# A random-feature attention with a routed two-layer network: h read once per block, y read one block later, a rewoven last step, and one-hots laid out in steps of one

## The chip, the cores and the metric

The kernel runs on one core of a Trainium2 chip. The metric is the device time of one execution in microseconds (us), as the median of several runs. TensorE is called PE in the profile, VectorE DVE, ScalarE ACT, GpSimd POOL and SyncE SP. "Line numbers" such as L926 are lines of the kernel before.

## The reference

Two stages. The first is attention with random features, for 8 batches, 8 heads, 576 positions and head dimension 64, with 128 features; its output, laid out as 4608 rows of 512, is the input of the second, a mixture of 8 experts of which each row takes the best one.

```python
def phi(x):
    proj = np.einsum('bhsd,md->bhsm', x, omega)
    return np.concatenate([np.cos(proj), np.sin(proj)], axis=-1) / np.sqrt(m)
q_p, k_p = (phi(q), phi(k))
kv = np.einsum('bhsm,bhsd->bhmd', k_p, v)
z = np.sum(k_p, axis=2)
num = np.einsum('bhsm,bhmd->bhsd', q_p, kv)
den = np.einsum('bhsm,bhm->bhs', q_p, z)
x = (num / den)            # 4608 rows of 512
...
logits = xn @ en.T / tau   # rows and expert embeddings normed
expert_idx = np.argmax(logits, axis=1)
gate_w = softmax(logits)[row, expert_idx]
for e in range(8):
    mask = expert_idx == e
    h = np.maximum(x[mask] @ w1[e], 0.0)          # 512 -> 1024
    out[mask] = gate_w[mask, None] * (h @ w2[e])  # 1024 -> 512
```

## The kernel before

**Attention loop.** There are 32 steps (a batch and a pair of heads each), software-pipelined by hand in the loop over n at L1067: step n makes the features of its own q (`proj_q`, L269; `whole_turns`, `frac`, `fold`, `wave`), the k features of step n+1 (`proj_k`), the sums of k features on POOL (`zsum`, L315), the products kv (`kv_products`, L327), and finishes step n-1: `kv_copy`, `kv_turn` (L350), `kv_out` (copy L374), `num` (L380, products L389) and `norm` (L397). `to_rows` and `store_rows` write the rows x to DRAM; `sums` (L455), `squares`, `square_sums` and `square_rows` (L444) prepare logits and norms. The loop runs to n = 32, where only the finishing half is left. Inside a step the order in each engine's queue is the order of the calls.

**Routing.** Rows are sorted by expert into blocks of 128 rows. This is done twice: once for the first half of the batches during steps 18 to 30 (`route_first`, L1009; its pieces go through a small holding list, `release`), giving blocks 0 to 10, and once for the rest while blocks 0 to 6 run (`route_second`, L1173, and `route_second_pe`). A routing goes: `choose`, `choose2` (best expert), `scan` (running counts), `rank` (two products, L632 and L633), `places` to `places3` (each row's block and row within it), `block_hot` and `row_hot` (one-hots of these), `invert` (36 products, L722, in the second one, that turn row numbers into a list of rows per block), `rows_of` and `block_experts`. Gates (`gates_a` to `gates_d`, with a tanh on ACT) are stored beside the rows. Most DVE operations of the routing have the helper's line: L153 in the blocks, L177 where they were held.

**Blocks.** Block j: `gather` (L819, an indirect DMA from POOL, issued four blocks ahead, three buffers) fetches the rows; `turn_x` transposes them on PE with a copy by ACT for blocks 0 to 2, and `turn_x_dma` (L856, from SP's queue) by DMA from block 3 on; `turn_x` also copies the gate (L852). `hidden(j)` (L921) makes h in two PSUM banks with 32 products L926, 16 for each bank, and ACT applies relu to each bank in an instruction of its own (L934, L936). `result(j)` (L941) makes y in one bank with 8 products L947, and ACT reads it with the gate as scale (L967). `scatter(j)` (L972, an indirect DMA from POOL) writes the rows of y to the output. h uses banks 4, 5 or 0, 1 and y bank 3 or 7, by the parity of j. The weights' addresses depend on the block's expert: PE holds them in 48 registers, which `place` (L908) sets by register adds, between the products of `result`.

`block` (L1223) calls, in this order: `hidden(j+1)`, `route_second_pe`, `turn_x(j+2)`, `turn_x_dma(j+3)`, `route_second`, `gather(j+4)`, `result(j)`, `scatter(j)`. So PE's queue has h of the next block in front of y of this one. 40 blocks are run always; the last 3 stand in a branch that this input doesn't take. `scatter(38)` and `scatter(39)` come after the branch.

The pieces that the change touches at the end of the loop:

```python
if n < NS:                      # L1085
    proj_q(n, place_first if n == NS - 1 else lambda: None)
...
if n == NS:                     # L1101
    hidden(0, "act")
if n > 0:
    kv_turn(n - 1)
    kv_out(n - 1)
release(100.0)
if n == NS:
    place(1, range(NW1))
```

`place_first` (48 adds) runs between the two groups of products of the last `proj_q`. In step 31 `route_first` also holds `choose(2)`, `square_rows(2)`, `choose2(2)`, which `release(100.0)` lets out after `kv_out`. The first gather is issued at the start of step 31, the gathers 1 to 3 at its end.

Of the kernel before, what the change touches and what calls it, by code (L numbers as in the profile page):

```python
# [28 lines left out]
def kernel(  # L29
# [12 lines left out]
    nc = tc.nc  # L42
# [95 lines left out]
    with tc.tile_pool(name="psA", bufs=1, space=PSUM) as psA, tc.tile_pool(  # L138
# [130 lines left out]
        def proj_q(n, between=lambda: None):  # L269
            d = st[n]  # L270
            for par in range(2):
                r0 = 64 * par
                nc.tensor.matmul(  # L273
                    qreg[:, 512 * par : 512 * par + 512],
                    lhsT=omT[r0 : r0 + 64],
                    rhs=d["qT"][r0 : r0 + 64, P:],
                    start=True,
                    stop=True,
                )
            between()  # L280
            nc.tensor.matmul(  # L281
                qreg[:, 1024:1152],
                lhsT=omT[64:P],
                rhs=d["qT"][64:P, 0:P],
                start=True,
                stop=True,
            )
# [414 lines left out]
        def block_hot(blk, ns, k0, nk, ar):  # L702
            bm = ar.take(ns * nk, BF16).rearrange("p (s k) -> p s k", k=nk)
            rr = ar.take(ns * nk * 2, BF16).rearrange("p (s t k) -> p s t k", t=2, k=nk)
            shp = [P, ns, nk]
            rv.tensor_tensor(
                bm, bc(io_p[:, k0 : k0 + nk], shp, 1), bc(blk, shp, 2), ALU.is_equal
            )
            rv.tensor_tensor(rr[:, :, 0], bm, bc(tok_hi[:, 0:ns], shp, 2), ALU.mult)
            rv.tensor_tensor(rr[:, :, 1], bm, bc(tok_lo[:, 0:ns], shp, 2), ALU.mult)  # L710
            return rr

        def row_hot(oh, lo, a, b):
            shp = [P, b - a, P]
            rv.tensor_tensor(
                oh[:, a:b], bc(io_p, shp, 1), bc(lo[:, a:b], shp, 2), ALU.is_equal
            )

        def invert(oh, rr, ns, nk, inv):
            inv = inv[:, 0 : 2 * nk]  # L720
            for s in range(ns):
                nc.tensor.matmul(  # L722
                    inv,
                    lhsT=oh(s),
                    rhs=rr[:, s].rearrange("p t k -> p (t k)"),
                    start=(s == 0),
                    stop=(s == ns - 1),
                )
            return inv
# [191 lines left out]
        def hidden(j, eng):  # L921
# [12 lines left out]
            nc.scalar.activation(hT[:, 0:512], h_ps[:, 0:512], AF.Relu)  # L934
            if eng == "act":
                nc.scalar.activation(hT[:, 512:], h_ps[:, 512:], AF.Relu)  # L936
            else:
                nc.vector.tensor_scalar(hT[:, 512:], h_ps[:, 512:], 0.0, None, ALU.max)
            d["hT"] = hT

        def result(j):  # L941
# [4 lines left out]
            for c in range(NW2):  # L946
# [14 lines left out]
                elif c == 6 and 0 < j < NBLK - 1:  # L961
                    place(j + 1, [NW1 + NW2 * ((j + 1) % 2) + 7])
            if j < NBLK - 1:
                y = late("si" + "kq"[j % 2], j // 2 % 2, 2 * D).bitcast(FP32)
            else:
                y = late("coq", 0, 2 * D).bitcast(FP32)
# [3 lines left out]
        ys = {}  # L970
# [38 lines left out]
        def route_first(n):  # L1009
# [43 lines left out]
            elif m == 12:  # L1053
                gates_d(0, GRP1)
                store_gates(0, GRP1)
            elif m == 13:
                choose(GRP1)
                square_rows(GRP1)
                choose2(GRP1)
# [7 lines left out]
        for n in range(NS + 1):  # L1067
# [13 lines left out]
            if n == NS - 1:  # L1081
                gather(0)
            if 0 < n <= n1 + 2:
                nc.tensor.addr_align(128, STEP_AT)
            if n < NS:  # L1085
                proj_q(n, place_first if n == NS - 1 else lambda: None)
# [13 lines left out]
            release(0.9 if n < NS - 1 else 0.0)  # L1100
            if n == NS:  # L1101
                hidden(0, "act")
# [3 lines left out]
            release(100.0)  # L1106
            if n == NS:
                place(1, range(NW1))
            if nx:
# [6 lines left out]
            if n > 2:  # L1116
# [7 lines left out]
            if n >= NS - 1:  # L1124
                turn_x(n + 1 - NS, "act")
# [17 lines left out]
            if n < NS:  # L1143
                kv_products(n)
                wave(n, "si", "q")
                wave(n, "co", "q")
            if n > 0:
                norm(n - 1)
            if n == NS - 2:
                load_v(n + 1)  # L1150
            route_pool(n)
            if n == NS - 1:
                gather(1)
# [8 lines left out]
        r2 = {}  # L1162

# [9 lines left out]
        def route_second(j):  # L1173
            if j == 0:
# [18 lines left out]
                )  # L1193
                choose(NGRP - 1)
                choose2(NGRP - 1)
                scan()
            elif j == 1:
                squares(NS - 1, nc.vector)
# [9 lines left out]
            elif j == 3:  # L1208
                r2["rr"] = block_hot(r2["blk"], NSLOT, K1, NBLK - K1, r2["a"])
            elif j == 4:  # L1210
                for a in range(0, 18, 6):
                    row_hot(r2["oh"][0], r2["lo"][:, 0:18], a, a + 6)
            elif j == 5:
                for part in (gates_a, gates_b, gates_c, gates_d):
                    part(GRP1, NGRP)
                store_gates(GRP1, NGRP)
                for a in range(0, 18, 6):
                    row_hot(r2["oh"][1], r2["lo"][:, 18:36], a, a + 6)
# [4 lines left out]
        def block(j, end):  # L1223
            if j + 1 < end:
                hidden(j + 1, "act")
# [12 lines left out]
            if not LAST - 2 <= j < LAST:  # L1238
                scatter(j)
# [6 lines left out]
        with tc.If(nb > LAST):  # L1246
            turn_x(LAST, "act")
            hidden(LAST, "act")
# [41 lines left out]
```

## Time and profile before

| what | before |
|---|---|
| median of 3 runs | 482.73 us (482.70, 482.73, 485.98) |
| the profiled execution | 485.38 us, span 483.5 us, mean granted PE clock 0.986 |
| attention loop, to the last num | 0 to 320.3 us |
| result(0) to result(7), start to start | 323.30 to 354.70 us |
| result(7) to result(39), start to start | 354.70 to 472.4 us |
| tail | the last product ends at 474.3 us, the span at 483.5 us |
| busy time | PE 456.8, PE weight load 379.5, POOL 367.2, ACT 340.3, DVE 294.7 us |

Times are of one profiled execution on the only core. In a timeline a row has start, length, engine, line, operation, output and inputs with their shapes and the number of instructions merged, and in brackets the idle time of the engine ahead of it with what ended it; "issue" means that the profile shows nothing that it waited for. Two blocks without a pause are 7.03 us (2 x 3.515).

### The profile page before, as it was taken

The page shows a single profiled execution, that of the slowest core. Times are in us where ns is not written, and L with a number is a line of the kernel's source. Part 1 is how long each engine was busy: PE and PEld are TensorE (multiplying, and loading weights), DVE is VectorE, ACT ScalarE, POOL GpSimd, SP SyncE. Part 2 cuts the span into 40 slices and gives each one's busy share as a digit, 9 for nine tenths or more (in the row PEclk, how much of TensorE's full clock was granted, in tenths as well). Part 3 has the DMA queues.
Part 4 walks back from the last instruction along what each step waited for, and adds up shares of the span by engine and source line. Part 5 has one row for each costly group of instructions (what it writes and reads, how often), then busy time and mean ns, then how long its engine had stood idle before and what let it go on. Part 6 is the DMA issues. An engine that isn't in the chain of part 4 may idle for free.

```text
span 483.5 us, 18511 instructions
## 1 busy us (share of the span) xinstructions
PE 456.8 (94%) x7778; PEld 379.5 (78%) x7778; DVE 294.7 (61%) x523; ACT 340.3 (70%) x439; POOL 367.2 (76%) x472
## 2 busy tenths in 40 slices
PE   8999999999999999999999899889899999999992
PEld 7888888898898888888888798767577676666660
DVE  4689888799888789989888988769710000000000
ACT  3878888888888889899889789464345354453541
POOL 3799888889999999989999789768645554645543
PEclk9999999999999999999999999899989999999997
DMA  6499798798887888897888868335636455454531
GB/s 179 103 186 205 170 173 167 186 166 163 176 165 144 204 165 160 164 169 168 166 160 184 153 143 130 64 66 136 137 97 145 136 116 138 122 131 137 125 95 35
DMA packets 77715, 70.46 MB, mean 146 GB/s; under 512 B 49461, under 2 KB 57653, under 8 KB 77632
## 3 DMA queue, kind: packets, MB, share of 16 engines
q0 software_dynamic: 18064, 30.96, 34.2%
q1 hardware_dynamic: 59168, 37.80, 32.6%
q8 instruction: 64, 1.05, 0.9%
q10 hardware_dynamic: 400, 0.49, 0.4%
q14 instruction: 19, 0.16, 0.1%
HBM read 67.90 MB, written 15.22 MB: 172 GB/s over the span
## 4 chain that ended last, share of the span: by engine, by line
PE 39%; POOL 27%; issue 19%; DVE 6%; DMA 4%; ACT 3%; POOLq 1%; SPq 0%; ACTq 0%; DVEq 0%
PE ps L389 11%; PE ps L335 9%; POOL xin_all L821 7%; PE ps L227 5%; PE ps L261 5%; POOL zt L322 4%; PE ps L273 4%; POOL out_dram L974 4%; DMA out_dram<-sik,prm 3%; POOL zt L323 2%; POOL zs L324 2%; POOL zs L325 2%; PE ps L364 2%; PE ps L356 2%; POOL lsq L774 2%
## 5 line engine op out<-in xcount | busy, mean ns | idle before, releaser
L926 PEld LDWEIGHTS <-w_sb 128*128 x1280 | 75.8, 98 | 18.9 <-issue 10.5
L926 PE MATMUL ps<-kq,w_sb 128*128 128x128 f16 x1280 | 81.5, 220 | 6.3 <-issue 4.7
L389 PE MATMUL ps<-kv,siq 128*64 128x73 f32 x1152 | 77.8, 231 | 1.5 <-ACT cok L934 0.6
L947 PE MATMUL ps<-w_sb,cok 128*128 x320 | 76.4, 383 | 0.5 <-ACT gpos L852 0.5
L389 PE MATMUL ps<-kv,coq 128*64 128x73 f32 x1152 | 76.2, 228 | 0.0
L389 PEld LDWEIGHTS ps<-kv,siq 128*64 128x64 f32 x1152 | 61.4, 137 | 5.3 <-issue 0.7
L389 PEld LDWEIGHTS ps<-kv,coq 128*64 128x64 f32 x1152 | 62.0, 139 | 0.0
L821 POOL DMA_INDIRECT xin_all<-rf_x,prm x43 | 46.5, 1081 | 14.2 <-issue 13.5
L322 POOL TENSOR_TENSOR zt<-sik 128x512 f32<-128x512 f32 x32 | 41.1, 1284 | 19.5 <-ACT sik L311 19.2
L936 ACT ACTIVATE cok<-ps 128x512 f16<-128x512 f32 x40 | 24.0, 601 | 44.8 <-PE ps L947 19.4
L947 PEld LDWEIGHTS <-cok 128*128 128x128 f16 x320 | 29.9, 98 | 29.6 <-issue 1.3
L323 POOL TENSOR_TENSOR zt<-zt 128x256 f32<-128x256 f32 x64 | 47.8, 747 | 5.0
L974 POOL DMA_INDIRECT out_dram<-siq,prm x20 | 20.2, 1008 | 40.8 <-ACT siq L967 39.6
L294 ACT ACTIVATE siq<-ps 128x1152 f32<-128x1152 f32 x32 | 36.2, 1131 | 17.3 <-PE ps L281 17.3
L298 DVE SCALAR_TENSOR_TENSOR sik<-sik,ps 128x1152 f32<-128x1152 f32 x32 | 43.2, 1349 | 4.1 <-ACT sik L294 4.0
L298 DVE SCALAR_TENSOR_TENSOR siq<-siq,ps 128x1152 f32<-128x1152 f32 x32 | 43.1, 1346 | 1.4 <-ACT siq L294 1.4
L322 POOL TENSOR_TENSOR zt<-cok 128x512 f32<-128x512 f32 x32 | 43.5, 1359 | 0.0
L294 ACT ACTIVATE sik<-ps 128x1152 f32<-128x1152 f32 x32 | 36.2, 1132 | 7.3 <-PE ps L261 4.6
L311 ACT ACTIVATE siq<-siq 128x1152 f32<-128x1152 f32 x32 | 37.1, 1159 | 5.2 <-DVE coq L304 5.2
L311 ACT ACTIVATE cok<-cok,consts 128x1152 f32<-128x1152 f32 x32 | 39.9, 1246 | 0.0
L311 ACT ACTIVATE coq<-coq,consts 128x1152 f32<-128x1152 f32 x32 | 39.8, 1244 | 0.0
L324 POOL TENSOR_TENSOR zs<-zt 128x128 f32<-128x128 f32 x64 | 34.9, 546 | 5.0
(198 smaller groups left out, 1131.1 us busy)
## 6 DMA issues: line engine op xcount, KB each, us to landing
w_sb<-in_moe_w_dram POOLq DMA_DIRECT2D x32, 512.0 KB
kq<-in_q_dram SPq DMA_DIRECT2D x62, 144.0 KB
kq<-in_k_dram SPq DMA_DIRECT2D x62, 144.0 KB
v<-in_v_dram SPq DMA_DIRECT2D x34, 144.0 KB
rf_x<-xb SPq DMA_DIRECT2D x32, 144.0 KB
xin_all<-in_v_dram SPq DMA_DIRECT2D x30, 144.0 KB
xin_all<-rf_x,prm POOLq DMA_INDIRECT x43
kq<-xin_all SPq DMA_TRANSPOSE x37
```

The costliest lines, as they stand in the source:

```text
L294: nc.scalar.activation(si, REG[nm], AF.Copy, bias=CMAGIC, scale=1.0)
L298: nc.vector.scalar_tensor_tensor(out=si, in0=si, scalar=CMAGIC, in1=REG[nm], op0=ALU.subtract, op1=ALU.subtract)
L311: nc.scalar.activation(t, t, AF.Sin, bias=pio2 if which == "co" else 0.0, scale=-TWO_PI * SINSC)
L322: nc.gpsimd.tensor_tensor(zt, t[:, 0:4], t[:, 4:8], ALU.add)
L323: nc.gpsimd.tensor_tensor(zt[:, 0:2], zt[:, 0:2], zt[:, 2:4], ALU.add)
L324: nc.gpsimd.tensor_tensor(z, zt[:, 0], zt[:, 1], ALU.add)
L335: nc.tensor.matmul(kreg[64 * half : 64 * half + 64, 512 * hh : 512 * hh + P], lhsT=d["v"][r0 : r0 + 64, c], rhs=ph[r0 : r0 + 64, s * P : s ...
L389: nc.tensor.matmul(nm2[r0 : r0 + 64, a, (c - c0) * W : (c - c0) * W + W], lhsT=ph[:, s * P + r0 : s * P + r0 + 64], rhs=d["kv"][:, half, h ...
L821: ins = nc.gpsimd.indirect_dma_start(out=t, out_offset=None, in_=x_rows[:], in_offset=bass.IndirectOffsetOnAxis(ap=prm[:, j : j + 1], axis=0),
L926: nc.tensor.matmul(h_ps[:, f * P : f * P + P], lhsT=weights(k), rhs=d["xT"][:, c * P : c * P + P], start=(c == 0), stop=(c == 3),)
L947: nc.tensor.matmul(y_ps, lhsT=d["hT"][:, c * P : c * P + P], rhs=weights(NW1 + NW2 * (j % 2) + c), start=(c == 0), stop=(c == NW2 - 1),)
L974: ins = nc.gpsimd.indirect_dma_start(out=out[:], out_offset=bass.IndirectOffsetOnAxis(ap=prm[:, j : j + 1], axis=0), in_=y, in_offset=None ...
```

## The change

1. **h.** `hidden` ends in one ACT instruction of 128x1024 over both banks; the parameter for another engine is gone.
2. **y.** The read of y is a function of its own, `rows_out(j)`, called in block j+1 after `hidden(j+2)`; the last two blocks of a series read their y at once. Block j scatters y of j-1.
3. **Last steps.** In step 31: gather 1 is issued with gather 0, `place_first` comes after `kv_out`, `choose(2)` before `kv_turn`, `turn_x(1)` at the end, `square_rows(2)` after `norm`. In step 32: `choose2(2)` at the start; `hidden(1)`, from block 0, follows `hidden(0)`, the kv turn and the adds, and stands before the last `num`. One `square_sums` goes from step 31 to step 32.
4. **One-hots.** `block_hot` makes its arrays with the row slot innermost, so that a two-input DVE operation has 16-bit operands in steps of one; the inversion reads its moving operand with a step of 36. In the second routing, ACT first copies the values that were read with step zero into the output's place (`wide_k`, and `wide_lo` in six pieces of 128x768), and DVE compares in place. The pieces are spread over blocks 3 to 5, with two of DVE's six after the gates and one between them.
5. **squares(31)** goes from DVE to ACT, into block 0.

```diff
-            nc.scalar.activation(hT[:, 0:512], h_ps[:, 0:512], AF.Relu)
-            if eng == "act":
-                nc.scalar.activation(hT[:, 512:], h_ps[:, 512:], AF.Relu)
-            else:
-                nc.vector.tensor_scalar(hT[:, 512:], h_ps[:, 512:], 0.0, None, ALU.max)
+            nc.scalar.activation(hT, h_ps, AF.Relu)
...
+            y_banks[j] = y_ps
+
+        def rows_out(j):
+            y_ps = y_banks.pop(j)
...
             if n == NS - 1:
                 gather(0)
+                gather(1)
...
-                proj_q(n, place_first if n == NS - 1 else lambda: None)
+                proj_q(n)
...
+            if n == NS - 1:
+                choose(GRP1)
             if n == NS:
-                hidden(0, "act")
+                choose2(GRP1)
+                hidden(0)
             if n > 0:
                 kv_turn(n - 1)
                 kv_out(n - 1)
             release(100.0)
+            if n == NS - 1:
+                place_first()
             if n == NS:
                 place(1, range(NW1))
+                hidden(1)
+                square_sums(n - 4)
...
-            if n >= NS - 1:
-                turn_x(n + 1 - NS, "act")
+            if n == NS - 1:
+                turn_x(0, "act")
...
+            if n == NS - 1:
+                turn_x(1, "act")
             if n > 0:
                 norm(n - 1)
+            if n == NS - 1:
+                square_rows(GRP1)
...
+        def wide_k(ns, k0, nk, ar):
+            bm = ar.take(ns * nk, BF16).rearrange("p (k s) -> p k s", s=ns)
+            nc.scalar.activation(bm, bc(io_p[:, k0 : k0 + nk], [P, nk, ns], 2), AF.Copy)
+            return bm
+
+        def wide_lo(oh, lo, a, b):
+            nc.scalar.activation(oh[:, a:b], bc(lo[:, a:b], [P, b - a, P], 2), AF.Copy)
+
+        def block_hot(blk, ns, k0, nk, ar, bm=None):
+            shp = [P, nk, ns]
+            wide = bm
+            if bm is None:
+                bm = ar.take(ns * nk, BF16).rearrange("p (k s) -> p k s", s=ns)
+                wide = bc(io_p[:, k0 : k0 + nk], shp, 2)
+            rr = ar.take(ns * nk * 2, BF16).rearrange("p (t k s) -> p t k s", t=2, s=ns)
+            rv.tensor_tensor(bm, wide, bc(blk, shp, 1), ALU.is_equal)
+            rv.tensor_tensor(rr[:, 0], bm, bc(tok_hi[:, 0:ns], shp, 1), ALU.mult)
+            rv.tensor_tensor(rr[:, 1], bm, bc(tok_lo[:, 0:ns], shp, 1), ALU.mult)
+            return rr.rearrange("p t k s -> p (t k) s")
+
+        def row_hot(oh, lo, a, b, wide=False):
             shp = [P, b - a, P]
             rv.tensor_tensor(
-                oh[:, a:b], bc(io_p, shp, 1), bc(lo[:, a:b], shp, 2), ALU.is_equal
+                oh[:, a:b], bc(io_p, shp, 1), oh[:, a:b] if wide else bc(lo[:, a:b], shp, 2), ALU.is_equal
             )
...
-                    rhs=rr[:, s].rearrange("p t k -> p (t k)"),
+                    rhs=rr[:, :, s],
...
             elif j == 3:
-                r2["rr"] = block_hot(r2["blk"], NSLOT, K1, NBLK - K1, r2["a"])
+                r2["rr"] = block_hot(r2["blk"], NSLOT, K1, NBLK - K1, r2["a"], r2["bm"])
+                wide2(0, 2)
             elif j == 4:
-                for a in range(0, 18, 6):
-                    row_hot(r2["oh"][0], r2["lo"][:, 0:18], a, a + 6)
+                wide2(2, 4)
+                hot2(0, 3)
             elif j == 5:
-                for part in (gates_a, gates_b, gates_c, gates_d):
-                    part(GRP1, NGRP)
+                wide2(4, 6)
+                gates_a(GRP1, NGRP)
+                gates_b(GRP1, NGRP)
+                hot2(3, 4)
+                gates_c(GRP1, NGRP)
+                gates_d(GRP1, NGRP)
                 store_gates(GRP1, NGRP)
-                for a in range(0, 18, 6):
-                    row_hot(r2["oh"][1], r2["lo"][:, 18:36], a, a + 6)
+                hot2(4, 6)
...
         def block(j, end):
-            if j + 1 < end:
-                hidden(j + 1, "act")
+            if 0 < j < end - 1:
+                hidden(j + 1)
+            if j - 1 in y_banks:
+                rows_out(j - 1)
...
             result(j)
-            if not LAST - 2 <= j < LAST:
-                scatter(j)
+            if j - 1 in ys and not LAST - 2 <= j - 1 < LAST:
+                scatter(j - 1)
+            if j + 2 >= end:
+                rows_out(j)
+                if j >= LAST:
+                    scatter(j)
```

`wide2(i0, i1)` and `hot2(i0, i1)` call `wide_lo` and `row_hot` on pieces i0 to i1 of six, three in each half of the one-hots.

## Prediction

> **What bounds the kernel now.** I read the page first, then stretches of the span, then the timelines of PE, DVE, ACT and POOL from 300 us on, since the change touches only the last two steps of the attention loop and the blocks. The page says that PE is the engine that matters (94% busy, against 70% for ACT and 61% for DVE), and its clock row has one dip, three quarters of the way through. Stretches:
>
> ```profile
> 303.01:304.17 1.16, 0.00 (x2) 0.01 (x1) 0.12 (x1) 0.39 (x1) 0.72 (x2) 1.00 0.56 103
> 305.95:309.36 3.41, 3.13 (x52) 3.16 (x54) 3.15 (x10) 2.70 (x3) 2.19 (x3) 0.51 0.45 70
> 312.78:316.19 3.41, 2.23 (x37) 2.08 (x38) 3.01 (x7) 1.93 (x2) 2.83 (x3) 1.00 0.10 20
> 346.92:350.32 3.40, 1.96 (x22) 1.14 (x23) 2.64 (x7) 0.69 (x2) 1.69 (x1) 0.99 0.85 128
> 350.32:353.73 3.41, 3.41 (x21) 2.16 (x19) 2.50 (x11) 0.69 (x1) 0.29 (x1) 0.50 0.34 39
> 354.70:472.40 117.70, 113.20 (x1251) 80.68 (x1249) 0.00 (x0) 56.83 (x125) 63.35 (x62) 1.00 0.49 125
> ```
>
> The columns are length, busy time of PE, weight load, DVE, ACT and POOL, clock, DMA share, GB/s. PE stands still from 303.01 to 304.17 (the register adds of place_first), and the clock is 0.51 from 305.95 to 309.36; it stands still for 1.4 of the 3.4 us before 350.32, and the clock is 0.50 after it. Yet 1.2 us idle of 3.4 (from 312.78) was not followed by a dip. Last, PE is idle for 4.5 us in the 33 blocks from 354.70 on.
>
> The pause before 350 is the second routing. PE's timeline:
>
> ```profile
> 346.05 0.69 PE L722 MATMUL ps<-ar,ohk 128*128 128x64 bf16 x18
> 346.90 0.53 PE L722 MATMUL ps<-ar,ohq 128*128 128x64 bf16 x5 [0.16 <-issue]
> 347.90 0.28 PE L722 MATMUL ps<-ar,ohq 128*128 128x64 bf16 x4 [0.47 <-issue]
> 348.64 0.42 PE L722 MATMUL ps<-ar,ohq 128*128 128x64 bf16 x9 [0.46 <-issue]
> 349.52 2.86 PE L947 MATMUL ps<-w_sb,cok 128*128 x8 [0.46 <-ACT gpos L852]
> ```
>
> The first 18 products of the inversion run at once; the other 18 come in pieces, because DVE is still making their one-hots:
>
> ```profile
> 343.86 0.24 DVE L153 TENSOR_SCALAR lsq<-lsq 128x144 f32<-128x144 f32 x1 [1.53 <-ACT lsq L153]
> 345.95 2.62 DVE L153 TENSOR_TENSOR ohq<-io_p,xa 128x768 bf16<-128x768 bf16 x3
> ```
>
> The 4.5 us in the blocks have another look. ACT, then POOL:
>
> ```profile
> 376.08 0.60 ACT L934 ACTIVATE cok<-ps 128x512 f16<-128x512 f32 x1 [1.15 <-PE ps L926]
> 379.23 0.60 ACT L936 ACTIVATE cok<-ps 128x512 f16<-128x512 f32 x1 [2.56 <-remote]
> 379.82 0.68 ACT L967 ACTIVATE siq<-ps,gpos 128x512 f32<-128x512 f32 x1
> ```
>
> ```profile
> 373.08 1.01 POOL L974 DMA_INDIRECT out_dram<-siq,prm  x1 [2.47 <-ACT siq L967]
> 374.39 1.03 POOL L821 DMA_INDIRECT xin_all<-rf_x,prm  x1 [0.30 <-issue]
> 375.72 1.02 POOL L974 DMA_INDIRECT out_dram<-sik,prm  x1 [0.30 <-issue]
> 377.05 1.03 POOL L821 DMA_INDIRECT xin_all<-rf_x,prm  x1 [0.30 <-issue]
> ```
>
> The products that L936 reads were over at 375.9, but it starts at 379.23, just after PE itself came out of a 0.63 us "issue" gap (at 379.08). This comes back every second block (386.85, 394.31, 401.84, ...), each time behind a row of scatter, gather, scatter, gather on POOL. The late L936 makes y late, y makes its scatter late, and that scatter then falls together with the next: the pattern feeds itself. What holds the release up I cannot see.
>
> **What the Trainium skill says.** "TensorE: Matmul & The Clock Gate", Part 1: PE runs at half clock after an idle window of some 3.4 us. The trace agrees on the length (3.41 us at 0.50) and shows a dip at 1.4 us idle in a window, none at 1.2. "VectorE: DVE Perf Modes", The perf-mode tier table: a two-input operation on 16-bit data runs at twice the rate if all steps are one. Before, one input has step zero: 1152 columns take 1.36 us, 768 take 0.94. No 16-bit two-input operation of before shows the doubled rate.
>
> **The change part by part**, against the profiled execution (485.38, span 483.5).
>
> *Last attention step.* place_first's 48 adds leave the 1.16 us gap and go between the kv turn and num, where PE waited 0.64 us for the copy L374 anyway; 0.5 stays exposed. choose moves into 2.5 us of idle DVE ahead of L374 (its 5 operations take 1.3 in block 0). So num (L389) runs 305.6 to 308.0 and not 306.23 to 310.13: its 3.9 us were 2.4 plus the slow clock. That gain is lost at once, as PE then waits for turn_x(0): L852 waited for the first gather until 309.74, and that gather is not issued earlier (POOL is on L462 until 303.7). The second gather, moved next to it, ends at 307.1 on POOL, where L322 started at 307.01, so the sums behind it are not late. SP's queue keeps its order. square_sums of step 28 and square_rows go to later places on DVE, 0.7 and 0.9 us; they stand behind norm or behind the kv copies, where DVE now has 1.4 us more to spare (fold and wave of q no longer wait behind choose). From 309.8: transposes 0.3, kv products 2.2, transposes 0.3, hidden(0) 1.8, kv turn 1.2, adds 0.5, hidden(1) 1.8. num of the last step starts at 317.9 (317.76 before). What is gained is that hidden(1) and one turn_x lie before it: result(0) starts at 320.6, not 323.30.
>
> *Wait put in its place.* The rank products need the scan, and the DVE chain from num's end to the scan's end takes 320.27 to 325.82, 5.5 us. PE now has only a turn_x (0.3), result(0) (1.72) and hidden(2) (1.79) to fill it: about 1.8 us idle at L632, in front of result(1) and all blocks behind. result(1): 326.3, not 327.06.
>
> *Second routing.* squares leaves DVE for ACT: 0.73. block_hot: 3 at 1.36 become 3 at 0.75 (the fixed part of 1.36 - 1152/0.96 = 0.16, plus half of 1.20): 1.8. row_hot: 6 at 0.94 become 6 at 0.55: 2.4. ACT takes on squares 0.68, one copy of 1152 (1.13, as L294) and six of 768 (0.60 + 256 x 0.83 ns = 0.81 each); these are in ACT's queue behind relu(j+1) and y, so the pair of block 5 cannot start before hidden(6) ends (340.3) plus relu 1.02 and y 0.6, and the tanh is behind it (344.0). Gates then need 2.2 and the last two row_hot 1.1: one-hots complete at 347.2, not 348.57. PE comes to L722 at about 344, idles for most of 2 us, and result(6) starts at 347.9: -1.6. The inversion's moving operand now has a step of 36 elements; the trace has no such read. Bounds: nothing, or 36 products at up to 0.07 more, 2.5 us; I take nothing. The first routing uses the same functions on 198 columns: its two products with the token numbers may lose 0.1 us each, in steps where DVE waits for PE; nothing. The half clock after the pause costs 1.7 now (L947 2.66 for 1.72, L926 2.52 for 1.79); with a pause near the 1.2 to 1.4 us border I take half of it back: -0.9, ends 0 and -1.7.
>
> *One read of h.* 0.60 + 512 x 0.83 ns = 1.02 for 0.48 + 0.60: nothing on PE's path, as result(j+1) comes 3.5 us after hidden(j+1).
>
> *y one block later.* y(j-1) waits for nothing then except relu(j+1), so scatters should come once per block, 3.5 us apart, each with one gather (2.35 us of POOL). The rows of four end, and with them the late releases. Ends: -4.5 and a loss (rival two). I take -3.5.
>
> Sum: -1.6 - 0.9 - 3.5 = -6.0; 485.4 becomes 479.4. The profiled execution was 2.65 above the median of 482.73, so the median becomes **476.7**. The tail behind the last product is unchanged: the last two y are still read at once, the last two scatters still follow the branch.
>
> **Rivals.** *One: the releases stay late, costing neither more nor less.* For it: I don't know their cause, and one pair at 353.44 and 354.76 was also followed by a late L936 (1.9 us). Then -2.5: 480.2. The same side holds the case that DVE gains no doubled rate: +4.2 on its chain, result(6) near 351, about 482.
>
> *Two: slower.* y(j-1) frees the PSUM bank that result(j+1) writes, and now stands behind relu(j+1). If that release stays 3.2 us late in every second block, relu starts at 379.23, y's read ends at 380.9, and L947 (380.09) waits 0.85: times 16 is 13.6 us, 493.8. It decides from about 1.8 us late on (3.5 less 1.02, 0.6 and hand-over). Against it: the lateness comes from y's own rhythm, which changes.
>
> **Chances.** Forecast 0.48, rival one 0.32, rival two 0.20. About 1% is what a measurement of this kernel can tell from no change: below 477.9 is faster, above 487.5 slower. The forecast's own range is 473 to 479.5; the whole, leaving a tenth out on each side, runs from 472 (all 4.5, all 1.7 and a shorter rank wait) to 488 (rival two in half of its blocks).
>
> **What would show it.** A gap of 1 to 2 us in front of L632; DVE's 768-column row_hot at 0.55; the clock row without the first dip; the read of h starting within 0.5 us of hidden's end in every block; POOL's scatters evenly spaced. An idle PE in front of L947 with y (ACT) as releaser would prove rival two; row_hot at 0.94, the case beside rival one.

## The result and the profile after

The changed kernel takes 496.65 us (median of 4 runs, 495.89 to 501.52), the kernel before 483.63 beside it: 1.028 times as long, 95% interval 1.021 to 1.036. The forecast was 476.7, at most 488. Two later comparisons, on two chips, gave 1.022 (1.016 to 1.027) and 1.023 (1.018 to 1.028). Ratios, and the medians of before given below for each chip, leave out executions over 1.5% longer than the fastest of the same kernel, which come with either kernel. The profiled execution took 496.77 us (span 495.0, mean clock 0.987); before it was 485.38 (483.5).

Lines have moved: h is made at L934, read at L942, y made at L951, read at L975, gathered at L829, scattered at L982; inversion L730, `num` L388, rank L631, wide copies L703 and L707. The stretches, with the same columns as before:

```profile
302.98:306.44 3.46, 2.56 (x22) 1.81 (x19) 2.86 (x9) 3.46 (x4) 2.32 (x5) 1.00 0.61 108
306.44:309.40 2.96, 2.62 (x72) 2.51 (x72) 2.93 (x2) 1.89 (x3) 2.63 (x3) 1.00 0.83 130
311.46:314.87 3.41, 3.41 (x72) 3.40 (x68) 1.81 (x5) 2.84 (x4) 3.18 (x5) 0.51 0.03 5
348.39:353.73 5.34, 4.46 (x40) 4.13 (x38) 2.91 (x7) 2.94 (x6) 2.60 (x3) 0.88 0.35 89
353.73:356.52 2.79, 2.79 (x10) 1.04 (x9) 2.34 (x8) 0.00 (x0) 0.22 (x1) 0.61 1.03 121
358.31:483.18 124.87, 114.12 (x1251) 81.68 (x1249) 0.00 (x0) 52.50 (x96) 64.38 (x63) 1.00 0.45 118
```

`num` (306.44 to 309.40) now runs at full clock, but the kv products behind it run at 0.51, and result(6), behind the inversion, still runs slow. The largest loss is the last row: from result(7) to result(39) 124.87 us, where before it was 117.70, with PE idle for 10.75 of them. PE's waits say for what:

```profile
PE ps L951 <- ACT siq L975: 11.2, 17, 2.3
PE ps L631 <- DVE cumx L153: 1.8, 1, 1.8
```

The first line (total, times, longest) is new: PE stands in front of the result products until ACT has read an older y. The longest wait, 2.3 us, is in front of result(39), ahead of which no products of a next `hidden` are left to do. In the traces with late releases the late reads fall at the end on odd blocks, so on 39 too, with one read of h, and on even ones with two reads; why, no run shows. ACT's timeline in two blocks, and POOL's ("remote" is a wait whose end the profile ties to no instruction):

```profile
379.96 1.02 ACT L942 ACTIVATE cok<-ps 128x1024 f16<-128x1024 f32 x1 [4.46 <-remote]
380.88 0.68 ACT L975 ACTIVATE siq<-ps,gpos 128x512 f32<-128x512 f32 x1
381.45 0.20 ACT L860 ACTIVATE gpos<-xin_all 128x1 f32<-128x1 f32 x1
381.54 1.02 ACT L942 ACTIVATE cok<-ps 128x1024 f16<-128x1024 f32 x1
382.45 0.70 ACT L975 ACTIVATE sik<-ps,gpos 128x512 f32<-128x512 f32 x1
```

```profile
381.84 1.00 POOL L982 DMA_INDIRECT out_dram<-siq,prm  x1 [1.92 <-ACT gpos L860]
383.15 1.03 POOL L829 DMA_INDIRECT xin_all<-rf_x,prm  x1 [0.30 <-ACT sik L975]
384.48 1.02 POOL L982 DMA_INDIRECT out_dram<-sik,prm  x1 [0.30 <-issue]
385.81 1.03 POOL L829 DMA_INDIRECT xin_all<-rf_x,prm  x1 [0.30 <-issue]
```

The products that the first relu reads had given way to the next result products at 377.38, so relu is 2.6 us late, with ACT idle: what came late is the release, the signal that PE's products may be read. y is read behind this relu until 381.56, and result (L951) starts at 381.61. Relus, ys and scatters still come in pairs, and POOL's rows of four are still there. In the second routing, PE and DVE:

```profile
348.39 2.32 PE L730 MATMUL ps<-ar,ohk 128*128 128x64 bf16 x18
350.53 0.90 PE L730 MATMUL ps<-ar,ohq 128*128 128x64 bf16 x6
352.31 1.60 PE L730 MATMUL ps<-ar,ohq 128*128 128x64 bf16 x12 [0.88 <-DVE ohq L153]
353.73 2.96 PE L951 MATMUL ps<-w_sb,cok 128*128 x8
```

```profile
337.34 0.76 DVE L153 TENSOR_TENSOR ar<-xa,tok_hi 128x1152 bf16<-128x1152 bf16 x1
...
345.68 0.56 DVE L153 TENSOR_TENSOR ohk<-io_p,ohk 128x768 bf16<-128x768 bf16 x1 [5.41 <-ACT ohk L707]
...
349.67 0.24 DVE L153 TENSOR_SCALAR lsq<-lsq 128x144 f32<-128x144 f32 x1 [2.00 <-ACT lsq L153]
```

DVE's operations have the forecast lengths (0.75 and 0.56), but DVE stands 5.41 us for a wide copy on ACT and 2.00 for the tanh; and 18 products of the inversion take 2.32 us, not 0.69.

The 11.5 us by which the spans of the two profiled executions differ (the medians differ by 13.0), by stretch: the last step begins 1.1 later (302.98 for 301.88; the other runs begin it anywhere from 301.7 to 303.1, with either kernel, and some at 304.8 to 309); from there to result(1) +0.4; result(1) to result(7) 29.8 for 27.6, +2.1; result(7) to result(39) +7.2; the end +0.7.

### The profile page after: what moved, and what is told of

Its sections match the earlier page's. It is cut to its first block, busy times and chain, and to the rows that moved or that the text cites. A ratio compares the mean times of both kernels' runs of the same rounds, so it can differ in the third digit from the quotient of the medians.

```text
span 495.0 us, 18403 instructions
## 1 busy us (share of the span) xinstructions
PE 461.3 (93%) x7778; PEld 384.2 (78%) x7778; DVE 291.0 (59%) x522; ACT 339.3 (69%) x407; POOL 366.3 (74%) x472
## 5 line engine op out<-in xcount | busy, mean ns | idle before, releaser
L942 ACT ACTIVATE cok<-ps 128x1024 f16<-128x1024 f32 x40 | 41.0, 1024 | 91.6 <-remote 78.2
L951 PE MATMUL ps<-w_sb,cok 128*128 x320 | 76.6, 383 | 11.2 <-ACT siq L975 11.2
L934 PEld LDWEIGHTS <-w_sb 128*128 x1280 | 74.9, 98 | 11.5 <-issue 2.4
L934 PE MATMUL ps<-kq,w_sb 128*128 128x128 f16 x1280 | 79.1, 219 | 1.4 <-DMA kq<-xin_all 0.6
L388 PE MATMUL ps<-kv,siq 128*64 128x73 f32 x1152 | 76.6, 229 | 1.2 <-issue 1.0
L388 PE MATMUL ps<-kv,coq 128*64 128x73 f32 x1152 | 75.0, 226 | 0.0
L388 PEld LDWEIGHTS ps<-kv,siq 128*64 128x64 f32 x1152 | 60.3, 135 | 5.2 <-issue 1.1
L951 PEld LDWEIGHTS <-cok 128*128 128x128 f16 x320 | 30.6, 98 | 42.2 <-issue 9.7
L388 PEld LDWEIGHTS ps<-kv,coq 128*64 128x64 f32 x1152 | 60.9, 137 | 0.0
L829 POOL DMA_INDIRECT xin_all<-rf_x,prm x43 | 44.4, 1034 | 19.5 <-issue 8.5
L982 POOL DMA_INDIRECT out_dram<-siq,prm x20 | 20.2, 1009 | 50.2 <-ACT gpos L860 43.6
L334 PE MATMUL ps<-sik,v 64*64 64x128 f32 x612 | 38.8, 280 | 0.0
L334 PE MATMUL ps<-cok,v 64*64 64x128 f32 x612 | 38.8, 280 | 0.0
```

The costliest lines, as they stand in the source:

```text
L334: nc.tensor.matmul(kreg[64 * half : 64 * half + 64, 512 * hh : 512 * hh + P], lhsT=d["v"][r0 : r0 + 64, c], rhs=ph[r0 : r0 + 64, s * P : s ...
L388: nc.tensor.matmul(nm2[r0 : r0 + 64, a, (c - c0) * W : (c - c0) * W + W], lhsT=ph[:, s * P + r0 : s * P + r0 + 64], rhs=d["kv"][:, half, h ...
L829: ins = nc.gpsimd.indirect_dma_start(out=t, out_offset=None, in_=x_rows[:], in_offset=bass.IndirectOffsetOnAxis(ap=prm[:, j : j + 1], axis=0),
L934: nc.tensor.matmul(h_ps[:, f * P : f * P + P], lhsT=weights(k), rhs=d["xT"][:, c * P : c * P + P], start=(c == 0), stop=(c == 3),)
L942: nc.scalar.activation(hT, h_ps, AF.Relu)
L951: nc.tensor.matmul(y_ps, lhsT=d["hT"][:, c * P : c * P + P], rhs=weights(NW1 + NW2 * (j % 2) + c), start=(c == 0), stop=(c == NW2 - 1),)
```

## The experiments

Each group of runs is on one chip, with its own runs of the kernel before. This turned out to matter: before took a median of 478.1 and 478.4 us on two of the chips, 484.4, 485.6 and 486.2 on three others. No chip comes in two groups, so the chip and the session on it are not told apart. I first blamed y's place in ACT's queue.

**First group: undoing one thing at a time.** `y_back` puts the read of y and its scatter back behind result(j):

```diff
-            if j - 1 in y_banks:
-                rows_out(j - 1)
...
+            rows_out(j)
+            if not LAST - 2 <= j < LAST:
+                scatter(j)
```

> The changed kernel with the read of y and its scatter put back behind result(j) in the same block; one read of h, the new last step and the new one-hots stay. Theory (late release held in ACT's queue): in every second block the release of the hidden products reaches ACT some 4.4 us late, relu stands in front of y in ACT's queue, and PE waits for the PSUM bank that y frees. With y in its old place PE's 17 waits in front of the result products, 11.2 us of which 2.3 at the very end, shrink to under 2 us, result(7) to result(39) takes 117 to 119 us and not 124.9, and the median falls by 5 to 8 us to about 489 to 491. Rival (one read of 1024 columns is the cause, as half of h can no longer start the result products early): the stretch stays at 123 to 126 us and the median within 1.5 us of 496.6.

`x_only` is the kernel before with the block part alone (the `hidden`, `rows_out` and `block` hunks of the diff).

> The kernel before with only the block part of the change: one read of h, and y read and scattered one block later; last step and one-hots as before. Theory (late release held in ACT's queue): this part alone costs what the stretch from result(7) to result(39) lost, 7 us, so the median goes from 483.6 to 489 to 492, with PE waiting 9 to 12 us for ACT's y in front of the result products. Rival (the loss needs the one-hots' changed queue on ACT or the drift of the last step): PE's waits for y stay under 3 us and the median within 2 us of 483.6.

`y_first` changes only the order of two calls:

```diff
+            if j - 1 in y_banks:
+                rows_out(j - 1)
             if 0 < j < end - 1:
                 hidden(j + 1)
-            if j - 1 in y_banks:
-                rows_out(j - 1)
```

> The changed kernel with y(j-1) read ahead of relu(j+1) in ACT's order; the scatter stays one block later. Theory (the order relu before y on ACT is what costs): PE's waits for y vanish (under 2 us in all), result(7) to result(39) takes 117 to 119 us, the median falls to 489 to 491, as in the kernel with y put back. Rival (the later scatter makes the bursts on GpSimd, and with them the late releases, worse): the stretch stays above 122 us and relu in front of the result products shows the waits that y showed.

`rr_rows` restores the order of `rr`, slot by slot, with DVE writing it in steps:

```diff
-            rr = ar.take(ns * nk * 2, BF16).rearrange("p (t k s) -> p t k s", t=2, s=ns)
+            rr = ar.take(ns * nk * 2, BF16).rearrange("p (s t k) -> p s t k", t=2, k=nk)
...
-                    rhs=rr[:, :, s],
+                    rhs=rr[:, s].rearrange("p t k -> p (t k)"),
```

> The changed kernel with the token one-hots written slot by slot, so that the moving operand of the inversion is contiguous again (64 columns in one row), and DVE writes them with a step. Theory (the step of 36 elements costs about 0.08 us per product): the 18 products of a row at once take 0.7 us and not 2.3, DVE's two products with the token numbers take 1.0 to 1.4 us and not 0.75, result(6) starts 1.5 to 2.5 us earlier against hidden(7), and the median falls by 1.5 to 2.5 us. Rival (the 2.3 us came from something else, such as half clock or the weight load): the products stay at 0.12 us each and the time within 0.7 us.

Ratios to before: `y_back` 1.002 (0.999 to 1.005), `x_only` 1.002 (0.998 to 1.006), `y_first` 0.999 (0.994 to 1.003), `rr_rows` 1.018 (1.011 to 1.025). In all four traces result(7) to result(39) takes 110.6 to 112.1 us, in whatever order y is read: from block 8 on, no relu begins more than 0.4 us after the products that it reads. So the block part costs nothing there, against my theory, and the first three tell nothing of its cause. `rr_rows` shows the operand's price, and a worse one beside it, on PE and on DVE:

```profile
347.28 0.69 PE L730 MATMUL ps<-ar,ohk 128*128 128x64 bf16 x18
348.75 0.35 PE L730 MATMUL ps<-ar,ohq 128*128 128x64 bf16 x6 [0.79 <-DVE ohq L153]
```

```profile
335.31 5.36 DVE L153 TENSOR_TENSOR ar<-xa,tok_hi 128x1152 bf16<-128x1152 bf16 x1
```

The contiguous products are back at 0.69 for 18, so the step of 36 elements is what costs. Start to start, the 18 took 2.14 us in the changed kernel (348.39 to 350.53, all at clock 1.00, so half clock is not the reason), 0.119 each for at most 0.038: 0.08 us, or 2.9 us over 36. But DVE writing with a step takes 5.36 us for 0.76, twice, and that is more than PE gains: the time did not fall by the expected 1.5 to 2.5 us, but is 1.8% above before where the three others are level with it.

**Second group: is the lateness in the kernel or in the chip?** The changed kernel, the kernel before, and `y_first` again, on one chip.

> The changed kernel as it is, once more, beside the next two on one chip. Four variants of it ran with no late release at all in their traces (ACT's relu waited for nothing but PE, blocks 3.51 us apart), where the changed kernel's own trace has 17 late ones. Theory (relu ahead of y in ACT's queue makes the lateness feed itself, whatever the place): the trace shows the 17 waits for y again, some 11 us, and the time is 2 to 3.5% above before. Rival (the late releases belong to the chip or the execution, and any order of y would show them there): where the kernel before runs without late reads of h, this one shows no wait for y either and stands at 1.00 to 1.01 of before.

> The kernel before as it is, profiled on the same chip as the changed kernel. Theory (the lateness is in the kernel's rhythm): relu's late starts of some 2.6 us in every second block are there as in its first trace, PE idle for about 4.7 us at issue in front of the hidden products. Rival (the lateness belongs to the chip or the execution): they are missing, PE's issue gaps in the blocks are under 1.5 us, and the time is 4 to 6 us below the 482.7 of its first runs.

> The changed kernel with y(j-1) read ahead of relu(j+1), again, beside the changed kernel on one chip. Theory (the order relu before y on ACT is what costs): no waits of PE for y, 12 to 16 us faster than the changed kernel beside it and level with before (0.995 to 1.003). Rival (lateness of the chip or the execution): within 2 us of the changed kernel, both with or both without late relus.

Changed kernel 494.1 us, ratio 1.022; PE's waits for y 9.6 us, 16 times. Before, profiled once, 483.56, issue gaps 3.0 us, stretch 117.5. `y_first` 489.1 us, ratio 1.014 (1.007 to 1.021): 5 us under the changed kernel, not the 12 to 16 of the theory. Its stretch is 118.1 (changed kernel 123.7), but result(1) to result(7) takes 32.4 us. On this chip the releases are late in all three. The lateness comes with the chip or the session on it; what it costs depends on the order.

**Third group, again on a chip with late releases.** The block part alone; the last step alone (`a_only`: before with the hunks of `proj_q`, `route_first`, `place_first` and the loop over n); `best_rr`: the changed kernel with y as in `y_back`, and with `block_hot` and `invert` of before, while `row_hot` keeps its wide copies:

```diff
-                r2["bm"] = wide_k(NSLOT, K1, NBLK - K1, r2["a"])
...
-                r2["rr"] = block_hot(r2["blk"], NSLOT, K1, NBLK - K1, r2["a"], r2["bm"])
+                r2["rr"] = block_hot(r2["blk"], NSLOT, K1, NBLK - K1, r2["a"])
```

And `no_scatter`, the changed kernel with

```diff
-            if j - 1 in ys and not LAST - 2 <= j - 1 < LAST:
-                scatter(j - 1)
```

> The kernel before with only the block part (one read of h, y read and scattered one block later), again, because the first time every release came on time in all kernels of that chip. Theory (late releases come with some chips; where they come, relu ahead of y on ACT turns each into a wait of PE): if the reads of h are late here (ACT's relu waiting for remote or for later PE lines), PE waits 8 to 12 us for y in front of the result products and the ratio to before is 1.010 to 1.020; if they are on time, the ratio is 0.995 to 1.005. Rival (the loss needs the one-hots' wide copies on ACT or the new last step): ratio under 1.006 even with late reads.

> The kernel before with only the last attention step rewoven (second gather, choose, place_first, hidden(1), square_sums and square_rows in their new places); blocks and one-hots as before. Theory (this part gains what result(1) gained in the second pair of traces, 2.65 us; I had put it at 0.76): result(1) starts 1 to 3 us earlier than before and the ratio is 0.993 to 0.998, with the rank wait of 1.8 us in front of it. Rival (the wait for the first gather brings a half clock in the kv products, as in the first trace after, and takes it all back): ratio 0.999 to 1.004.

> The changed kernel with y read and scattered in its own block again, and with the token one-hots made as before, slot by slot (contiguous moving operand, DVE at 1.36 for each of the three), while row_hot keeps its wide copies. Theory (y's place costs 7 us where releases are late, the strided operand some 3.3 us): the 36 products of the inversion take 0.04 us each again, PE has no waits for y, and the ratio to before is 0.992 to 0.999. Rival (the wide copies in ACT's queue are the larger loss in the routing, since ACT holds them behind the late relu): result(6) is no earlier than in the changed kernel, ratio 1.003 to 1.010.

> The changed kernel without the scatters of the blocks (blocks 0 to 33 never write their rows of out; the last ones do). Theory (GpSimd's back-to-back indirect transfers hold PE's releases up): with one gather per block, 3.5 us apart, relu starts within 0.5 us of hidden's end in every block, PE's waits for y vanish and blocks come every 3.5 us: 7 us or more below the changed kernel. Rival (the lateness comes from elsewhere, such as the gathers or PE's own queue): late relus and PE's waits for y stay in about every second block, and the time is within 2 us of the changed kernel. If the chip of this call shows no late reads in any kernel, the run tells nothing on this.

The block part: ratio 1.013 (1.005 to 1.021), 5.6 us, PE waiting 10.8 us for y, 16 times: here it costs. The last step: 0.995 (0.991 to 0.999), 3.2 us gained. `best_rr`: 1.017 (1.008 to 1.026), so its rival is right, and more. In the routing result(1) to result(7) takes 31.0 us with contiguous operands too, as PE waits 3.8 us for one-hots. DVE makes the last two of these behind the gates and waits 6.49 us for the tanh of the gates, which stands in ACT's queue behind a late relu (ACT is idle for 4.38 us ahead of it) and two wide copies. And y is in its own block, yet the stretch is 123.6 us: PE now waits for relu (5.0 us, 12 times, put down to the gate copy just behind it, and 2.3 at the end). `no_scatter`: 0.976 (0.968 to 0.983). Its stretch, then ACT's waits for the hidden products (total, times, longest):

```profile
358.94:469.76 110.82, 110.80 (x1251) 80.43 (x1249) 0.00 (x0) 54.06 (x95) 31.93 (x32) 1.00 0.31 66
```

```profile
ACT cok L942 <- PE ps L934: 73.4, 38, 7.8
```

Not one relu waits for "remote" (18 times in the changed kernel), PE has no idle time, and the stretch is the one of the other kind of chip. So on this chip the releases were late only with the scatters among POOL's transfers. Their writes are gone with them (66 GB/s in the stretch for 118 in the changed kernel), and whether POOL's instructions or this traffic held the releases up, the run does not tell.

**Fourth group: the halves of the block part, the one-hots alone, the gathers.**

`x_read` is before with only the hunk of `hidden`, `x_late` before with only those of `rows_out` and `block`, `c_only` before with only those of the one-hots and of `route_second`. `no_gather` is the changed kernel with

```diff
+            if j >= 8:
+                nc.sync.dma_start(out=t, in_=x_rows[P * (j - 8) : P * (j - 7)])
+                xin[j] = t
+                return
```

> The kernel before with only the one read of h (one relu of 1024 columns for two of 512); y stays in its block. Theory one (the later y is what costs): no change, ratio 0.997 to 1.004, the stretch from result(7) to result(39) as before, 115 to 118 us. Theory two (two reads hide a late release: the first half's release is posted 0.9 us earlier and lets half of the result products start, one read gives that up): PE waits for relu in front of the result products for 5 to 8 us, the stretch is 121 to 124 us, the ratio 1.010 to 1.018. On a chip with releases on time both say no change.

> The kernel before with only y one block later (read behind relu(j+1), scattered one block later); h is still read in two halves. Theory one (the later y is what costs): PE waits for y 8 to 12 us, stretch 122 to 125 us, ratio 1.010 to 1.018, as with both halves of the block part. Theory two (the one read is what costs): waits for y under 4 us, stretch 115 to 119 us, ratio 0.997 to 1.005. On a chip with releases on time both say no change.

> The kernel before with only the one-hots' part (16-bit steps of one, wide copies on ACT, squares on ACT, strided operand in the inversion). Theory (the strided operand costs 36 products at 0.08 us, and the wide copies stand behind late relus on ACT): inversion products at 0.12 us, DVE waits 3 us or more for the wide copies, result(7) starts 2 to 5 us later than before's, ratio 1.004 to 1.012. Rival (DVE's shorter one-hots pay for it, as I had forecast): result(7) no later than before's, ratio 0.994 to 1.001.

> The changed kernel with the gathers of blocks 8 and later as plain copies of consecutive rows on SP's queue (the rows are not those that the routing chose, so the blocks work on other tokens than they should); the scatters stay on GpSimd, one per block. Theory one (a crowd of indirect transfers back to back holds PE's releases up): with one scatter per 3.5 us there is no crowd, relus are on time, PE's waits for y vanish, 8 us or more below the changed kernel. Theory two (the scatters themselves do it): late relus and waits for y stay, within 3 us of the changed kernel. On a chip with releases on time it tells nothing.

This chip had its releases on time: `x_read` 0.998 (0.995 to 1.000), `x_late` 1.000 (0.997 to 1.002), and neither tells the halves apart. `c_only`: 1.012 (1.003 to 1.021), so the one-hots seem to cost something even here, but its trace doesn't show where: result(1) to result(7) takes 26.9 us, 24.8 in `x_late`'s, but also 26.8 in `x_read`'s, which has the old one-hots. `no_gather` (1.027) is inconclusive: its copies on SP's queue stand in the way of the transposing transfers (PE waits 10.7 us for those), and the chip couldn't show late releases.

**Fifth group, on a chip with late releases.** The halves again, and the changed kernel.

> The kernel before with only the one read of h, again. If relus are late here: theory one (the later y is what costs) says ratio 0.997 to 1.004 and a stretch from result(7) to result(39) of 115 to 118 us; theory two (two reads hide part of a late release) says waits of PE for relu of 5 to 8 us, a stretch of 121 to 124 us, ratio 1.010 to 1.018. If relus are on time: ratio 0.996 to 1.001 as on the chip before, and nothing told.

> The kernel before with only y one block later, again, h read in two halves. If relus are late here: theory one (the later y is what costs) says 8 to 12 us of PE waiting for y, a stretch of 122 to 125 us, ratio 1.010 to 1.018; theory two (the one read) says waits under 4 us, 115 to 119 us, ratio 0.997 to 1.005. If relus are on time: ratio 0.997 to 1.003, and nothing told.

> The changed kernel as it is. Where relus are late: ratio 1.018 to 1.030 as in its first two measurements, some 11 us of waits for y. Where they are on time: no waits for y, blocks 3.51 us apart, and only the last step (about -3 us) and the one-hots (+1 to +6 us) are left: ratio 0.996 to 1.008. Rival (the changed kernel brings the lateness with it on any chip): ratio above 1.015 while the kernel before runs at 479.

One read alone: 1.010 (1.004 to 1.017). Later y alone: 1.000 (0.996 to 1.004). Changed kernel: 1.023. The stretch from result(7) on, one read first, then the later y:

```profile
360.44:487.02 126.58, 115.53 (x1251) 81.77 (x1249) 0.06 (x1) 53.99 (x95) 64.79 (x64) 1.00 0.47 120
```

```profile
354.57:470.94 116.37, 114.23 (x1251) 81.12 (x1249) 0.16 (x1) 55.83 (x126) 63.45 (x63) 1.00 0.49 126
```

(The profiled execution of `x_read_2` took 499.88 us, where the ratio rests on three of 490.0 to 491.5; its last step begins 6 us late. `best_rr`, one read too, has 123.6 without that.) With one read PE is idle for 11 us; two of its waits in front of the result products (L943 in that kernel), of which the longest, 2.4, is again in front of result(39):

```profile
PE ps L943 <- ACT gpos L852: 3.4, 8, 0.8
PE ps L943 <- ACT cok L934: 2.4, 1, 2.4
```

Another 3.4 us are issue gaps in front of the hidden products, which before has too.

Theory two holds, and mine falls: by itself the one read costs, and the later y doesn't. When both are there, y stands last in ACT's queue and the profile names y, but what holds ACT up is the late relu. Then y's place counts as well: `y_first_2` has one read too, but y ahead of relu, and its stretch is 118.1 where the changed kernel beside it has 123.7.

How these go together can be estimated from the traces. PE wants h, and the bank of y, 3.5 us after the last hidden product; with two reads it wants the second half of h 0.86 later, at 4.4. The table gives how long after the end of its products the last read of h begins (median of the blocks from 7 on where this is over 1 us), what ACT has to do from there, when that is done by this sum, and how long PE waited in front of result(8) to result(38), in us:

| kernel | h late by | ACT then reads | done at | wanted at | PE waited |
|---|---|---|---|---|---|
| before | 3.0 | half of h, 0.60 | 3.6 | 4.4 | 0 |
| x_late_2 | 2.5 | half of h, then y, 0.60 + 0.6 | 3.7 | 3.5 | 1.1 |
| y_first_2 | 2.4 | h, 1.02 | 3.4 | 3.5 | 2.4 |
| x_read_2 | 3.0 | h, 1.02 | 4.0 | 3.5 | 4.5 |
| changed, first trace | 2.5 | h, then y, 1.02 + 0.6 | 4.1 | 3.5 | 8.0 |

The waits grow with what the sum exceeds, except for `y_first_2`; its late reads begin 2.0 to 2.7 us late, so that some of them miss the 3.5. The lateness itself isn't the same: its median is 2.4 to 2.6 in the six late traces with y one block later, 2.7 to 3.0 in the five with y in its own block. Why, no run shows.

The stretches, in us, side by side:

| kernel | releases | last step to result(1) | result(1) to (7) | result(7) to (39) |
|---|---|---|---|---|
| before, two traces | late | 25.2, 26.4 | 27.6, 25.0 | 117.7, 117.5 |
| changed, three traces | late | 25.5, 23.5, 25.6 | 29.8, 31.1, 31.6 | 124.9, 123.7, 126.6 |
| x_only_2 (block part) | late | 24.9 | 26.1 | 124.7 |
| x_read_2 / x_late_2 | late | 26.6 / 26.4 | 25.7 / 25.5 | 126.6 / 116.4 |
| a_only (last step) | late | 23.4 | 28.2 | 115.0 |
| y_first_2 / best_rr | late | 23.8 / 23.5 | 32.4 / 31.0 | 118.1 / 123.6 |
| x_only / x_late | on time | 24.6 / 24.6 | 25.4 / 24.8 | 110.8 / 110.6 |
| c_only (one-hots) | on time | 26.0 | 26.9 | 110.8 |

## Why the prediction was wrong, by its own steps

**One read of h: the step that failed.** It was put at "nothing on PE's path, as result(j+1) comes 3.5 us after hidden(j+1)". That is true of a release on time (110.6 to 112.1 us in the traces of two chips), but the trace of before showed them some 3 us late in every second block, at most 3.3 (products over at 375.9, L936 at 379.23). Two reads bear that: the first half is read on time, half of the result products can start, and the second half is needed 0.86 us (half of 1.72) after the first. One read of 1.02 us that begins 3.3 late ends 4.3 after hidden, later than 3.5. The two numbers stood side by side in my text, and I used the lateness against y but not against h. The bearing by halves is argued from these numbers and fits the estimates above. Shown is that the one read costs by itself where releases are late (1.010), and that y's place behind it adds to that in the changed kernel, in the one pair of traces that tells it (123.7 for 118.1).

**y one block later, with its end of the late releases: -3.5 forecast, +7.2 measured.** The rows of four on POOL did not end: pairs of late relus make pairs of ys, and these make pairs of scatters, also one block later. By itself this part did nothing (1.000). What I hoped for, releases on time, does come without the scatters, and is worth more than I had said: 117.7 to 110.8 is 6.9 us, since besides the 4.5 us of idle time PE's busy time has 2.4 more (113.20 for 110.80).

**Rival two** had the sign and what the profile names, 17 waits of PE for y: 11.2 us in the trace, 13.6 in its sum. But its reason, y's place, was only half of it; it gave the one read 1.02 us of its budget and did not see that this was the price. All that stood against it was that the rhythm might change.

**Second routing: -1.6 forecast, a loss in the traces** (29.8 to 31.6 us from result(1) to result(7) in the changed kernel, 25.0 to 28.2 in the six late traces with the old one-hots). Three terms. DVE's lengths were right: 0.75 and 0.55 forecast, 0.75 and 0.56 measured, as the Trainium skill has it ("VectorE: DVE Perf Modes", The perf-mode tier table, and for the steps What auto-detection actually checks: twice the rate for 16-bit operands in steps of one). The strided operand, "I take nothing", took 2.9 us, above even my upper bound of 2.5. The wide copies wait on ACT behind late relus: I had them follow a relu on time, DVE waited 5.41 us for them and 2.00 for the tanh behind them, and the one-hots were complete at 352.7, not 347.2. Where relus are on time, these waits were 2.14 and 2.47 (`c_only`).

**Half clock after the inversion: -0.9 forecast, nothing measured.** result(6) takes 2.96 us, as before (2.86). The border between 1.2 and 1.4 us of idle time, read from two windows, did not hold. In the first stretch below, from the trace of before itself, PE is idle for 1.63 of 3.41 us, and the clock stays at 1.00 behind it; in the second, from `y_first_2`, PE is never idle, and half clock follows (353.98 to 357.39):

```profile
268.37:271.78 3.41, 1.78 (x27) 1.39 (x27) 3.41 (x5) 2.26 (x4) 3.10 (x6) 1.00 0.98 124
```

```profile
350.57:353.98 3.41, 3.41 (x29) 3.13 (x27) 1.21 (x5) 0.00 (x0) 0.00 (x0) 1.00 0.69 118
```

`y_back`, `no_scatter` and `no_gather` show the same as `y_first_2`. In all four PE runs the slow products of the inversion there, but `y_first` and `c_only` run them too and have no half clock behind them. What sets it off stays open.

**Last attention step: right in mechanism, its gain larger or nothing.** The gap of 1.16 us is gone, `num` starts at 306.44 (forecast 305.6, on a start 1.1 us earlier) and PE waits 1.43 us for the first gather, as forecast. The half clock moved rather than went: the kv products at 0.51 cost 1.7 us of 3.41 in this trace, and result(0) came at 322.84 for 320.6. In the second trace of the changed kernel, with a wait of 1.3 us at the same place, the clock stayed at 1.00, and result(0) came at 319.74. Alone, this part gains 3.2 us; its trace has full clock there and 23.4 us from the last step to result(1), for 25.2 and 26.4 before. The rank wait was forecast at 1.8 us and is 1.76.

**The sum.** Predicted -6.0: the blocks +7.2 for -3.5, result(1) to result(7) +2.1 for -1.7 (half clock included), the way to result(1) +0.4 for -0.8, and 1.8 us at the start and the end that the change was not charged with. `a_only` is the only version of the whole computation with an interval below 1 (0.995, 0.991 to 0.999); its gain is under 1%.

## What to carry to other kernels

Before merging two reads of a PSUM tile into one, look how late the release before them comes in the trace, not only how long the reads take: the second read may be what keeps a late release off the critical path. A layout that doubles VectorE's rate must be priced on every engine that reads it too, and on the queue that makes it. When the profile names the last instruction of an engine's queue as releaser, look at what that engine waited for in front of it. And one chip is not enough for a change of 1%: the block part alone measured 1.002 on one chip and 1.013 on another.

## What the runs showed of the hardware

- PE's releases came late in the blocks on some chips (before: 484.4 to 486.2 us there) and on time on others (478.1, 478.4). Four versions, each traced once on either kind, show it with the same program: 110.6 to 110.9 us from result(7) to result(39) where releases are on time, 116.4 to 126.6 where they are late. Before itself was traced only where they are late. Without the scatters they came on time on a chip where they were late. Why, and by which path, no run shows.
- A moving operand of 64 columns in steps of 36 16-bit elements takes 0.119 us per product at full clock, a contiguous one at most 0.038.
- DVE writing 1152 16-bit elements in steps of 64 elements takes 5.36 us, in steps of one 0.76.
- Half clock is not the same in each execution of a kernel: the kv products ran at 0.51 and 0.50 in two traces of the changed kernel (3.4 us each), at 1.00 in a third. It came behind 3.41 us without any idle time of PE in four traces, and stayed away behind 3.41 us with 1.63 idle in the trace of before.
